# A planner's rule for short transfers beside weight loads, and the constants of a list schedule set anew

## The chip, the cores and the metric

The kernel runs on one core of a Trainium2 chip. The metric is the device time of one execution in microseconds (us), the median over several runs. Before the change it is 965.49 us (three runs, 964.73 to 967.22).

## The reference

Eight batches of local attention with a few global positions, and behind them a two-layer feed-forward network with a Mish-like function. Cut to what matters:

```
k_all, v_all = concat(k_g, k_l), concat(v_g, v_l)          # 32 global + 512 local positions, 8 heads of 64
out_g = softmax(q_g k_all^T / 8) v_all                     # global queries see everything
s_ll  = where(|i - j| <= 32, q_l k_l^T / 8, -1e9)          # local queries: a band of 65 ...
out_l = softmax([q_l k_g^T / 8, s_ll]) [v_g; v_l]          # ... and the 32 global keys
x = concat(out_g, out_l) as (8 * 544) rows x 512
h = x @ w_in (512 x 2048);  g = h * tanh(softplus(h));  result = g @ w_out (2048 x 512)
```

The weights arrive as 8-byte floating-point numbers (512 KB for a piece of 128 x 512) and are turned into 4-byte ones on the core. The matrix products are made with pairs of 16-bit numbers (a high and a low part of each operand), three products for one.

## The kernel before, in words

The attention is cut into 128 units: a batch b, a pair of heads hp and a quarter t of the 512 local queries. A unit takes scores on TensorE (`scores`, L621), the masked maximum on VectorE (`row_max`, L635), the exponential on ScalarE (`expo`, L644), a split into high and low parts, a transpose, and the product with V (`pv`, L717), whose result VectorE scales (`x_norm`, L727). The rows are then transposed for the network (`xh`, `xl`). For batch 0 the transposes run on TensorE; from batch 1 on they are DMA transposes.

The product with V needs the V rows in a shifted layout. `v_move` makes it: eight transfers from on-chip memory to on-chip memory for each pair of heads, of 32, 128, 48, 96, 48, 48, 16 and 16 KB, all issued by the sync engine (SP) into the tiles `va` and `vc`. The last three come from `vgf`, the global part.

The network works on 17 blocks of 256 rows (two for each batch, and one of all global rows), eight steps to a block. A step is `m1_mm` (L853, 24 matmuls into `h`), Mish on ScalarE (L896), the split of the result on VectorE (L343, L909), and `m2_mm` (L921, twelve matmuls into `o`).

The weights come in 32 pieces: 0 to 15 of `w_in` (W1), 16 to 31 of `w_out` (W2). Pieces 0 to 4 are loaded by ScalarE's queue, the others by GpSimd's (POOL). Piece k of W1 lands in one of five staging slots, slot k % 5, so piece k + 5 can only be loaded when VectorE has turned piece k (three instructions: `w_bits` L427, `w_sum` L434 and L436). TensorE then makes statistics (`w_stat`, L448). When all 16 pieces are in, `w_norm` (L455) finds the common scale, and `w_split` makes the high and low parts that `m1_mm` and `m2_mm` read. So the first `m1_mm` needs all of W1 turned, and the attention rows of the first half of batch 0.

All instructions are put in order ahead of time by a list scheduler (`Plan.order`). Each task has an engine, a cost in ns, what it depends on, and a rank. The scheduler keeps a model of time for TensorE, VectorE, ScalarE, POOL and SP, and at each step takes the task that can start first, on equal starts the one of lowest rank. The instructions are then emitted in that order, and each engine works off its own list strictly in order: a task whose input is late holds up all behind it on its engine. No rank or cost of the planner is seen by the chip; they only set the order.

The rank is the task's number in the order in which the program names it, or, where `pl.slot` is set, 37 times that slot. The network's tasks get `BOOST` added (`pl.late`), so they yield to attention tasks with which they compete. `S1` says in which slot (one slot is one unit of attention) each step of the network is named: blocks 0 to 3 by `BLOCKS` and `PACE`, blocks from 4 on one step a slot with a lag of `LAGX`. `CONV1`, `RATE1`, `CONV2`, `RATE2` set the slots of the turning of the weights, `FIRST1`, `STEP1`, `FIRST2`, `STEP2` those of their splits, `AHEAD_DMA` how far ahead of its turning a piece's load is ranked, `LOAD1` and `LOADS1` the ranks of the opening loads.

In the planner's model, weight loads occupy a line of their own that ends at `late`, and SP's transfers one that ends at `moved`. A transfer starts at s, costs ns = KB x 2.81, and where the two lines overlap each is made longer by the other (`both`). SP issues at least 620 ns apart (`DMA_MIN`); a transfer is taken as landed 2300 ns after it has left its line. A piece of weights costs 512 x 2.81 = 1439 ns on its line. The lines that the change touches:

```
if e == DMA:
    s = max(moved, t)
    both = min(ns, max(0, late - s - self.DMA_IN))
    late += both
    moved = s + ns + both
```

Of the kernel before, what the change touches and what calls it, by code (L numbers as in the profile page):

```python
# [27 lines left out]
NF = 8  # L28
# [21 lines left out]
class Plan:  # L50
# [7 lines left out]
    LOYAL = 800  # L58
    TABLE = 1283
    COLD = 2  # L60
    DEEP, ISSUE, SOFT, LANES = 5, 450, 600, 8

    def __init__(self):
        self.tasks = []
# [70 lines left out]
    def order(self):  # L135
        N = len(self.tasks)
        left, users = [0] * N, [[] for _ in range(N)]
        for n, t in enumerate(self.tasks):
            both = t[2] | t[3]
            left[n] = len(both)  # L140
            for d in both:
                users[d].append(n)
        free = dict.fromkeys((PE, DVE, ACT, POOL, DMA), 0)
        free[POOL], pool = 6900, "dma"
        queue = {e: [] for e in free}
        start, done, on = [None] * N, [0] * N, [None] * N
        columns = {}
        moved, far, late, hard, soft = 0, [], 0, [], []

        def tensor(t, ns, rows):  # L150

            while ns > 1e-6:
                k = int(t / self.TICK + 1e-9)
                slow = 1 if columns.get(k - 1, 0) >= self.COLUMNS else self.COLD
                d = min(ns * slow, (k + 1) * self.TICK - t)
                columns[k] = columns.get(k, 0) + d * 2.4 * rows
                ns -= d / slow
                t += d
            return t

        def enter(n):
            engs, fn, deps, after, new, pri, rows, table = self.tasks[n]
            for e, ns in engs:
                t = max([done[d] + (self.NEXT[e] if on[d] == e else self.HOP) for d in deps] + [start[a] for a in after] + [0])
                bisect.insort(queue[e], (pri, n, ns, t))

        def first(e):

            best = None
            for pri, n, ns, t in queue[e]:  # L170
                table = self.tasks[n][7]
                t = max(t, free[e])
                if table == "dma":
                    lane = hard if e == ACT else soft
                    t = max(t, far[-self.DEEP] if len(far) >= self.DEEP else 0, lane[-self.LANES] if len(lane) >= self.LANES else 0)
                elif e == DMA:
                    t = max(t, hard[-self.LANES] if len(hard) >= self.LANES else 0)
                elif e == ACT and table not in (None, self.table):
                    t += self.TABLE
                e0 = self.tasks[n][0][0][0]  # L180
                if e0 != e and free[e0] <= t + self.LOYAL:
                    continue
                if best is None or t < best[0]:
                    best = (t, pri, e, n, ns)
                    if t == free[e]:
                        break
            return best

        for n in range(N):
            if not left[n]:  # L190
                enter(n)
        for _ in range(N):
            t, pri, e, n, ns = min(c for c in map(first, free) if c)
            if e == POOL:
                pool = self.tasks[n][7]
            start[n], on[n] = t, e
            if self.tasks[n][7] == "dma":
                s = max(t + self.DMA_IN, late)
                both = min(ns, max(0, moved + self.DMA_IN - s))
                moved += both  # L200
                late = s + ns + both
                far.append(late)
                free[e] = t + (self.ISSUE if e == ACT else self.SOFT)
                done[n] = far[-1] + self.DMA_OUT
                (hard if e == ACT else soft).append(done[n])
                queue[e] = [c for c in queue[e] if c[1] != n]
                for u in users[n]:
                    left[u] -= 1
                    if not left[u]:
                        enter(u)  # L210
                continue
            if e == ACT:
                self.table = self.tasks[n][7] or self.table
            for x, _ in self.tasks[n][0]:
                queue[x] = [c for c in queue[x] if c[1] != n]
            if e == PE:
                ns = tensor(t, ns, self.tasks[n][6]) - t
            if e == DVE and free[POOL] > t and pool != "dma":
                ns += 0.6 * min(ns, free[POOL] - t)
            if e == DMA:  # L220
                s = max(moved, t)
                both = min(ns, max(0, late - s - self.DMA_IN))
                late += both
                moved = s + ns + both
                free[e] = max(t + max(self.DMA_MIN, self.tasks[n][6]), moved - self.DMA_AHEAD)
                done[n] = moved + self.DMA_IN + self.DMA_OUT
                hard.append(done[n])
            else:
                free[e] = done[n] = t + ns
            for u in users[n]:  # L230
                left[u] -= 1
                if not left[u]:
                    enter(u)
        self.start, self.on, self.done = start, on, done
        return sorted(range(N), key=lambda n: (start[n], n))
# [13 lines left out]
def attn_mish_kernel(ctx: ExitStack, tc: tile.TileContext, qt, kt, vm, vg, qg, w1, w2, consts_in, out, w64):  # L249
# [314 lines left out]
    def v_hi(b, hp):  # L564
        vf = ("vf", b, hp)
        pl.add([(ACT, act(512) + 93), (DVE, dve2(512))], 0, lambda e: scaled(e, X[vf][:, :, 0, :], X["vraw", b][:, hp], X["sv", b][:, 1:2]), r=[("vraw", b), ("sv", b)], new=[("vf", vf)])
# [198 lines left out]
    def g_max(b, hp):  # L765
        mx = ("gmx", b, hp)
        pl.add(DVE, 69 + 1.04 * 272, lambda: V.tensor_reduce(
            out=X[mx][:, 0:1], in_=X["g", b, hp][:, :272], axis=AX.X, op=ALU.max), r=[("g", b, hp)], new=[("gmx", mx)])

        def go():  # L770
            across(X[mx], 0)
            V.tensor_scalar(X[mx][:, 2:3], X[mx][:, 0:1], X[mx][:, 1:2], -SCALE, ALU.max, ALU.mult)  # L772
        pl.add(DVE, 330, go, w=[mx])
# [175 lines left out]
    UNITS.sort(key=lambda x: (x[0], x[2] // 2, x[1], x[2]) if x[0] < HALVED else x)  # L949
    steps = [(blk, i) for blk in range(NBLK) for i in range(NF)]  # L950

    BLK2 = 29.169
    BLK3 = 39.967
    LAGX = 19.225
    BLOCKS = [9, 17, max(25, int(BLK2)), max(33, int(BLK3))]
    PACE = 0.79
    S1 = [int(BLOCKS[s // NF] + PACE * (s % NF)) if s < 4 * NF else s + max(18, int(LAGX)) for s in range(len(steps))]
    LAG2 = 2
    LATER = 24
    BOOST = 84.202  # L960

    def at(u):
        return [x for x, v in zip(steps, S1) if v == u]

    def unit(u):
        return UNITS[u] if 0 <= u < NU else None
# [3 lines left out]
    def slot(u):  # L970
# [5 lines left out]

        m, m2, md = (at(u - k) for k in (0, LAG2, LAG2 + 1))
        fu, bu, vu = unit(u + 1), unit(u), unit(u - 1) if u - 1 < LATER else unit(u - 2) if u - 2 >= LATER else None
# [24 lines left out]
        if mv1 and t == (2 if hp == 3 else 1):  # L1003
            v_hi(*n1)
        pl.late = BOOST
        for x in m[:1]:
            m1_mm(*x, 0)
        pl.late = 0
        if t == 2:
            g_scores(b, hp)  # L1010
            g_max(b, hp)
        pl.late = BOOST
        for x in m:
# [24 lines left out]
        if mv1 and t == (2 if hp == 3 else 1):  # L1038
            v_lo(*n1)
        pl.late = BOOST  # L1040
        for x in m2:
# [4 lines left out]
        if t == 3:  # L1046
            g_pv(b, hp)
        pl.late = BOOST
        for x in m2:
# [38 lines left out]

    LAG = 4
    ORDER = "k0 q0 m w0 b w1 w2 k1 q1 w3 w4 k2 q2 k3 q3 g"  # L1090
    LOAD1 = -7.91
    LOADS1 = 0.038
    CONV1 = 1.096
    RATE1 = 0.0
    CONV2 = 2.335
    RATE2 = 0.514
    FIRST1 = 6.564
    STEP1 = 1.0
    FIRST2 = 6.491
    STEP2 = 0.0  # L1100
    AHEAD_DMA = 12.457

    def weights():
        for k in range(32):
            at = CONV1 + RATE1 * k if k < 16 else CONV2 + RATE2 * (k - 16)
            if k >= 5:
                pl.slot = at - AHEAD_DMA
                w_load(k)
            pl.slot = at
            w_bits(k)  # L1110
            w_sum(k)
            if k % 16 >= LAG:
                w_stat(k - LAG)
            if k % 16 == 15:
                pl.slot = -100
                for i in range(k - LAG + 1, k + 1):
                    w_stat(i)
                w_norm(k // 16)
        pl.slot = None
        pl.settle()  # L1120
# [3 lines left out]
    for i, x in enumerate(ORDER.split()):  # L1124
        a, n = x[0], int(x[1:] or 0)
        pl.slot = LOAD1 + LOADS1 * i
        if a == "w":
# [17 lines left out]
    weights()  # L1145
    splits += [(FIRST1 + STEP1 * j, j) for j in range(8)] + [(FIRST2 + STEP2 * j, 8 + j) for j in range(8)]
    splits.sort()
    for u in range(-1, max(S1[-1] + LAG2 + 2, NU + 3)):
        slot(u)
# [57 lines left out]
```

## Time and profile before

| what | value |
|---|---|
| median of three runs | 965.49 us (964.73 to 967.22) |
| the profiled execution: its own time, its span | 969.12 us, 967.3 us |
| mean granted TensorE clock | 0.986 |
| busy: TensorE, VectorE, ScalarE, POOL | 916.4, 571.6, 553.6, 26.8 us |

The profile is of one execution, 3.63 us above the median of the runs; its span is 1.82 us shorter than its own time, which holds the start and the end outside the first and last instruction. Times in the trace are counted from the span's start. In lists of instructions the first number is the start, the second the duration; in square brackets stands how long the engine sat idle before, and what released it. In tables by stretch each engine has its busy time and its count of instructions, then come the granted TensorE clock, the mean share of the 16 DMA engines that was busy, and what they moved.

### The profile page before, as it was taken

The page shows a single profiled execution, that of the slowest core. Times are in us where ns is not written, and L with a number is a line of the kernel's source. Part 1 is how long each engine was busy: PE and PEld are TensorE (multiplying, and loading weights), DVE is VectorE, ACT ScalarE, POOL GpSimd, SP SyncE. Part 2 cuts the span into 40 slices and gives each one's busy share as a digit, 9 for nine tenths or more (in the row PEclk, how much of TensorE's full clock was granted, in tenths as well). Part 3 has the DMA queues.
Part 4 walks back from the last instruction along what each step waited for, and adds up shares of the span by engine and source line. Part 5 has one row for each costly group of instructions (what it writes and reads, how often), then busy time and mean ns, then how long its engine had stood idle before and what let it go on. Part 6 is the DMA issues. An engine that isn't in the chain of part 4 may idle for free.

```text
span 967.3 us, 20582 instructions
## 1 busy us (share of the span) xinstructions
PE 916.4 (95%) x8044; PEld 625.2 (65%) x8044; DVE 571.6 (59%) x1749; ACT 553.6 (57%) x1161; POOL 26.8 (3%) x52
## 2 busy tenths in 40 slices
PE   2569999999899999999999999999999999999997
PEld 1346657667577666666666766676666666666664
DVE  5599887767676775755566555755565552222222
ACT  1446886767676687766676657756775651211111
POOL 5111000000000000000000000000000000000000
PEclk9789999999999999999999999999999999999999
DMA  9865235675877976766465447644553321000000
GB/s 369 278 201 189 65 86 134 131 161 136 182 156 136 183 159 135 170 115 122 86 173 110 110 94 163 125 112 98 116 94 64 85 43 34 22 1 22 1 22 22
DMA packets 214417, 113.74 MB, mean 118 GB/s; under 512 B 181168, under 2 KB 194608, under 8 KB 213296
## 3 DMA queue, kind: packets, MB, share of 16 engines
q1 hardware_dynamic: 209568, 95.39, 44.7%
q0 software_dynamic: 3888, 14.16, 4.1%
q10 hardware_dynamic: 864, 2.88, 0.8%
q8 instruction: 63, 1.03, 0.4%
q14 instruction: 34, 0.28, 0.1%
HBM read 46.32 MB, written 8.91 MB: 57 GB/s over the span
## 4 chain that ended last, share of the span: by engine, by line
PE 81%; DVE 8%; DMA 7%; ACT 2%; issue 1%; SPq 1%; POOL 0%; ACTq 0%; DVEq 0%
PE o L921 34%; PE h L853 34%; PE s L621 5%; PE U L717 4%; PE g L755 2%; PE gu L809 2%; DVE W L434 1%; DMA pt<-ph 1%; DVE W L436 1%; DMA vgraw<-in_vg 1%; DMA gpt<-gph 1%; DMA W<-in_w 1%; DMA va<-vgf 1%; DMA consts<-in_consts 1%; DVE vmx L521 1%
## 5 line engine op out<-in xcount | busy, mean ns | idle before, releaser
L921 PE MATMUL o<-W,G 128*128 128x512 f16 x1632 | 386.3, 379 | 0.6 <-DVE W L498 0.5
L853 PE MATMUL h<-xh,W 128*128 128x256 f16 x2048 | 375.9, 273 | 0.2 <-ACT W L334 0.2
L853 PEld LDWEIGHTS <-W 128*128 128x128 f16 x3264 | 310.9, 98 | 72.6 <-issue 10.4
L853 PE MATMUL h<-xl,W 128*128 128x256 f16 x1024 | 279.6, 273 | 0.0
L921 PEld LDWEIGHTS <-G 128*128 128x128 f16 x1632 | 154.5, 98 | 151.3 <-issue 3.3
L896 ACT ACTIVATE e<-h,c 128x512 f32<-128x512 f32 (+1 forms) x137 | 93.2, 684 | 167.8 <-PE h L853 145.4
L343 DVE TENSOR_SCALAR G<-e,c 128x512 f16<-128x512 f32 (+1 forms) x137 | 66.1, 482 | 178.9 <-ACT e L896 177.9
L644 ACT ACTIVATE P<-P,nm 128x192 f32<-128x192 f32 (+1 forms) x256 | 117.4, 459 | 56.4 <-DVE nm L635 55.6
L635 DVE CUSTOM_DVE_ANT_0 P<-s,consts 128x192 f32<-128x192 f32 (+1 forms) x256 | 87.0, 369 | 37.1 <-PE s L621 32.1
L909 DVE SCALAR_TENSOR_TENSOR G<-e,c,G 128x512 f16<-128x512 f32 (+1 forms) x137 | 102.1, 745 | 3.4
L664 DVE SCALAR_TENSOR_TENSOR ph<-P,ph 128x384 f16<-128x384 f32 (+1 forms) x112 | 64.5, 589 | 37.0 <-ACT ph L341 35.2
L717 PEld LDWEIGHTS <-pt 96*128 96x128 f16 (+1 forms) x1536 | 61.5, 98 | 30.9 <-issue 12.4
L621 PE MATMUL s<-k,q 64*128 64x192 f32 (+1 forms) x512 | 65.7, 373 | 15.0 <-DMA q<-in_qt 13.4
L896 ACT ACT_TABLE_LOAD x56 | 71.8, 1283 | 5.3 <-PE h L853 4.3
L717 PE MATMUL U<-va,pt 128*128 128x64 f16 (+1 forms) x768 | 56.4, 194 | 14.3 <-DMA va<-vgf 8.0
L621 PEld LDWEIGHTS s<-k,q 64*128 64x128 f32 x512 | 44.0, 192 | 31.3 <-issue 23.8
L341 ACT ACTIVATE ph<-P 128x384 f16<-128x384 f32 (+1 forms) x99 | 51.4, 539 | 12.0 <-DMA pt<-ph 10.9
L717 PE MATMUL U<-vc,pt 96*128 96x64 f16 x768 | 55.8, 193 | 0.0
L644 ACT ACTIVATION_READ_ACCUMULATOR P<-P,nm 128x1 f32 x256 | 47.9, 187 | 0.0
L777 ACT ACT_TABLE_LOAD x22 | 28.2, 1283 | 26.7 <-DVE gmx L772 24.8
L644 ACT ACT_TABLE_LOAD x33 | 42.3, 1283 | 0.6
L341 ACT ACTIVATE ob<-o,c 128x512 f32<-128x512 f32 (+1 forms) x34 | 22.8, 672 | 25.8 <-PE o L921 25.7
(114 smaller groups left out, 713.1 us busy)
## 6 DMA issues: line engine op xcount, KB each, us to landing
k<-in_kt SPq DMA_DIRECT2D x32, 320.0 KB, 3.5
W<-in_w POOLq DMA_DIRECT2D x17, 512.0 KB, 7.4
out<-ob SPq DMA_DIRECT2D x33, 256.0 KB, 2.3
q<-in_qt SPq DMA_DIRECT2D x32, 256.0 KB, 3.1
vraw<-in_vm SPq DMA_DIRECT2D x8, 1024.0 KB, 5.9
wraw<-in_w POOLq DMA_DIRECT2D x10, 512.0 KB, 4.2
vc<-vf SPq DMA_DIRECT2D x32, 128.0 KB, 2.5
va<-vf SPq DMA_DIRECT2D x32, 96.0 KB, 2.6
```

Of the source, the lines that this page charges most:

```text
L341: A.activation(out=dst, in_=src, func=AF.Copy, scale=c)
L343: V.tensor_scalar(dst, src, c, None, ALU.mult)
L621: T.matmul(X[s[h]][:, cols(u)], X[q][r, u * 128:(u + 1) * 128], X[k][r, c0:c0 + w], start=True, stop=True)
L635: pl.add(DVE, 155 + 1.04 * w, lambda: V.tensor_tensor_reduce(out=half(P, h, w), in0=X[s][:, cols(t)], in1=mask[:, m0:m0 + w], scale=-SCALE ...
L644: pl.add(ACT, 460, lambda: A.activation(out=half(P, h, w), in_=half(P, h, w), func=AF.Exp, bias=X[nm], scale=-1.0, accum_out=X[sums][:, t, ...
L664: pl.add(DVE, dve(n), lambda: V.scalar_tensor_tensor(p_part(X[ph], t, 1), p_src(X[P], t), PSC, p_part(X[ph], t, 0), ALU.mult, ALU.subtract ...
L717: T.matmul(X[u][:, t, h, :], X[pt][:k, p * 4 + h * 2 + c, :], X[vx][:k, t, vl, h * 64:(h + 1) * 64], start=(n == 0), stop=(n == 5))
L777: pl.add(ACT, 470, lambda: A.activation(out=X[P], in_=X["g", b, hp][:, :272], func=AF.Exp, bias=X[mx][:, 2:3], scale=SCALE, accum_out=X[s] ...
L853: T.matmul(X[h][:, f * TB:(f + 1) * TB], wh(i, wl)[:, off:off + 128], X[x][:, d, o:o + TB], start=(n == 0), stop=(n == 11))
L896: chain(blk, i, ACT, 705, lambda a, z: A.activation(out=X[e][:, a:z], in_=hv(blk, i)[:, a:z], func=AF.Mish, bias=0.0, scale=X[c][:, 0:1]), ...
L909: chain(blk, i, DVE, 668, lambda a, z: V.scalar_tensor_tensor(gp(1, blk, i)[:, a:z], X[e][:, a:z], X["c", blk][:, 2:3], gp(0, blk, i)[:, a ...
L921: T.matmul(X[o], gp(g, blk, i)[:, f, t * 128:(t + 1) * 128], wh(8 + i, wl)[:, f * 512:(f + 1) * 512], start=(i == 0 and n == 0), stop=(i = ...
```

## The change

The planner gets a constant SHORT of 500 ns. While the line of the weight loads reaches more than 500 ns beyond a transfer's start on SP (after the 1300 ns of `DMA_IN`), that transfer costs at least 500 ns; since `both` then holds the same 500 ns again, it takes up 1000 ns of SP's line, and the loads' line is made 500 ns longer. Fifteen constants of ranks and slots have new values. An assertion on the order of steps emits nothing. No instruction is added, removed or resized: only the order in which the engines work may change.

```
-    DEEP, ISSUE, SOFT, LANES = 5, 450, 600, 8
+    DEEP, ISSUE, SOFT, LANES, SHORT = 5, 450, 600, 8, 500
...
             if e == DMA:
                 s = max(moved, t)
+                if late - s - self.DMA_IN > self.SHORT:
+                    ns = max(ns, self.SHORT)
                 both = min(ns, max(0, late - s - self.DMA_IN))
...
-    BLK2 = 29.169
-    BLK3 = 39.967
-    LAGX = 19.225
+    BLK2 = 31.263
+    BLK3 = 37.663
+    LAGX = 18.379
...
-    PACE = 0.79
+    PACE = 0.732
...
+    assert all(a <= z - (n % NF == NF - 1) for n, (a, z) in enumerate(zip(S1, S1[1:])))
...
-    BOOST = 84.202
+    BOOST = 122.269
...
-    LOAD1 = -7.91
-    LOADS1 = 0.038
-    CONV1 = 1.096
-    RATE1 = 0.0
-    CONV2 = 2.335
-    RATE2 = 0.514
-    FIRST1 = 6.564
+    LOAD1 = -9.482
+    LOADS1 = 0.109
+    CONV1 = 1.292
+    RATE1 = 0.142
+    CONV2 = 2.956
+    RATE2 = 0.457
+    FIRST1 = 6.031
     STEP1 = 1.0
-    FIRST2 = 6.491
-    STEP2 = 0.0
-    AHEAD_DMA = 12.457
+    FIRST2 = 5.526
+    STEP2 = 0.179
+    AHEAD_DMA = 11.972
```

## The prediction

> **What bounds the kernel now.** The page says which engine fills the span, and in which slices it does not: TensorE is busy in 95%, and what it lacks lies almost all in the first slices of 24 us, where its granted clock is also below full.
>
> ```profile
> PE 916.4 (95%) x8044; PEld 625.2 (65%) x8044; DVE 571.6 (59%) x1749; ACT 553.6 (57%) x1161; POOL 26.8 (3%) x52
> PE   2569999999899999999999999999999999999997
> PEclk9789999999999999999999999999999999999999
> ```
>
> So the span is 916.4 us of TensorE work and some 51 us in which it stood still, and a change of order can win or lose only such idle time. The table by stretch says what is short there.
>
> ```profile
> 37.00:44.00 7.00, 1.51 (x27) 1.50 (x27) 0.03 (x1) 0.00 (x0) 0.00 (x0) 0.50 0.84 251
> 44.00:63.00 19.00, 12.53 (x102) 8.05 (x101) 17.35 (x42) 5.64 (x14) 1.87 (x4) 0.77 0.64 186
> 63.00:81.00 18.00, 15.53 (x123) 8.63 (x120) 17.70 (x57) 11.40 (x28) 2.89 (x6) 0.97 0.54 187
> 81.00:140.00 59.00, 55.28 (x469) 37.76 (x466) 52.52 (x149) 45.88 (x85) 3.68 (x7) 1.00 0.38 106
> ```
>
> From 37 to 44 us neither VectorE (0.03 us) nor ScalarE does anything, and TensorE starts again only at the end. From 44 to 81 VectorE is full (35.05 of 37 us) and TensorE is not: what VectorE lost before 44 is missing there. The waits and the chain that ended last say what all waited for.
>
> ```profile
> PE U L717 <- DMA va<-vgf: 8.0, 1, 8.0
> 34.59 7.87 DMA va<-vgf
> 42.49 1.45 PE U L717 x24
> 36.02 0.69 DVE L434 SCALAR_TENSOR_TENSOR W<-W 128x512 int32<-128x512 int32 x1
> 43.97 0.43 DVE L727 TENSOR_TENSOR x<-U,rs 128x256 f32<-128x256 f32 x1 [7.25 <-PE U L717]
> ```
>
> One transfer of `v_move` (16 KB, for the first pair of heads) is issued at 34.59 and lands 7.87 us later. The first `pv` stands at the head of TensorE's list, `x_norm` at the head of VectorE's, and behind that the last third of the turning of piece 9. The planner had put them there because it thought the rows would be in.
>
> **The rule for short transfers.** What the planner believes, and what the trace has:
>
> ```profile
> 26.95 0.57 SPq L330 DMA_DIRECT2D va<-vf  x1
> 27.62 0.53 SPq L330 DMA_DIRECT2D vc<-vf  x1
> 28.97 1.76 SPq L330 DMA_DIRECT2D va<-vf  x3
> 30.77 0.59 SPq L330 DMA_DIRECT2D vc<-vf  x1
> 31.81 4.28 SPq L330 DMA_DIRECT2D va<-vgf  x3
> va<-vgf SPq DMA_DIRECT2D x64, 16.0 KB, 1.8
> va<-vgf SPq DMA_DIRECT2D x8, 16.0 KB, 4.2
> ```
>
> The last two rows are the same kind of transfer over the whole span and in the window 26 to 60: 1.8 and 4.2 us to landing. The old planner gives a 16 KB transfer 45 ns, so eight of them are its 620 ns spacing, 4.96 us. With the rule each takes 1.0 us of line while the loads' line reaches far enough, 8.0 us. So the new plan has the rows of a pair 8 x (1.0 - 0.62) = 3.0 us later. Does the condition hold when they are issued? These are the loads on POOL:
>
> ```profile
> 23.88 0.53 POOL L414 DMA_DIRECT2D wraw<-in_w  x1
> 26.33 0.53 POOL L411 DMA_DIRECT2D W<-in_w  x1 [1.91 <-DVE W L427]
> 29.60 0.53 POOL L411 DMA_DIRECT2D W<-in_w  x1 [2.75 <-DVE W L436]
> 34.27 0.53 POOL L411 DMA_DIRECT2D W<-in_w  x1 [3.58 <-DVE W L427]
> 36.06 0.53 POOL L411 DMA_DIRECT2D W<-in_w  x1 [1.26 <-DVE W L427]
> 45.40 0.54 POOL L411 DMA_DIRECT2D W<-in_w  x1 [8.81 <-DVE rs L726]
> DMA to landing us min/median/max: 3.4/7.1/9.0
> ```
>
> One load moves the line by 1.44 us, so alone it holds the condition for less than 1 us after its issue; but each raised transfer lengthens it by 0.5. I replayed the rule by hand at the trace's times (the load at 23.88 and two shortly before it already hold the line): it held for about seven of the first ten transfers. So it bites, not always.
>
> What can the hole take in? VectorE had that third of piece 9 waiting, and pieces 10 and 11, whose loads (26.33, 29.60) land by 35.3 and 38.6 at the latest time of the row above (9.0). Piece 12 (34.27) lands at 41.4 by the median of 7.1, piece 13 (36.06) at 43.2. In the dense stretch a piece costs the distance between two of its first instructions:
>
> ```profile
> 55.30 0.42 DVE L427 TENSOR_SCALAR W<-W 128x512 int32<-128x512 int32 x1
> 56.84 0.42 DVE L427 TENSOR_SCALAR W<-W 128x512 int32<-128x512 int32 x1
> 62.37 0.28 DVE L455 CUSTOM_DVE_ANT_0 wd<-ws,consts 128x128 f32<-128x128 f32 x1
> 80.90 0.27 PE L853 MATMUL h<-xh,W 128*128 128x256 f16 x1
> ```
>
> 1.54 us. So 0.7 + 2 x 1.54 = 3.8 us of work are surely at hand, 5.3 us with piece 12. The load at 45.40 (piece 14) waits for VectorE too: turned at 37, piece 9 frees its slot 8 us sooner, so the loads would not run dry behind it. The price of this edit is therefore a gain between 3.0 us (the planner's shift alone) and 7.25 us (the whole hole). I take 4.5, between the 3.8 and the 5.3, since the order that a planner with half the true lateness writes will use some of that work and not all. It counts in full for the end: W1 is complete at 62.37, the first `m1_mm` is at 80.90, and VectorE is full to there; from 81 to 140 TensorE lacks only 3.7 us, so an early start is not used up by a later wait of the same size. If that cover is gone (the filler sits elsewhere in VectorE's list) the gain is nothing.
>
> [...]
>
> **The ranks of the weights.** The turning of W1 moves from slot 1.10 for all pieces to 1.29 + 0.142 k: 7 ranks later for piece 0, (1.292 + 2.13 - 1.096) x 37 = 86 for piece 15. W2 starts 23 ranks later and ends 9 earlier; W1's splits come half a slot sooner. VectorE has the same instructions in another order. With 35.05 of 37 us busy the sum cannot move, only which of them are in first. Bounds: a slot of attention work on VectorE ahead of the last pieces (2.8 us, worked out below) later, the same earlier; I take 0. The opening loads keep their order on their queues: 0. The loads on POOL only change ranks among themselves: 0, within the same bounds.
>
> **The blocks.** Blocks 0 and 1 keep their slots but for one step each; block 2 goes from slot 29 to 31, block 3 from 39 to 37, all from block 4 on one slot sooner (19 to 18). `BOOST` goes up by 38 ranks, one slot of 37: from block 4 on the two cancel. Blocks 0, 1 and 2 yield more: one, one and three slots. What such a slot costs if TensorE cannot fill it is read from the steady part:
>
> ```profile
> 200.00:300.00 100.00, 95.98 (x954) 66.41 (x953) 66.96 (x234) 68.73 (x165) 0.65 (x1) 1.00 0.72 155
> 200.00:300.00 100.00, 39.65 (x336) 31.58 (x336) 1.00 0.72 155
> 200.00:300.00 100.00, 37.26 (x162) 15.02 (x161) 1.00 0.72 155
> 200.00:300.00 100.00, 8.77 (x72) 5.90 (x72) 1.00 0.72 155
> 200.00:300.00 100.00, 7.94 (x18) 1.00 0.72 155
> 200.00:300.00 100.00, 8.99 (x12) 1.00 0.72 155
> ```
>
> All; then the lines L853, L921, L621 (72 score matmuls, four to a unit: 18 units), L343 and L909. Attention alone takes (95.98 - 39.65 - 37.26) / 18 = 1.1 us of TensorE and (66.96 - 7.94 - 8.99) / 18 = 2.8 us of VectorE a unit. Without a network step beside it a unit would leave TensorE idle for 1.7 us. Today it is idle for 4.0 us in this stretch. The bounds are -4.0 (all of that gone) and 5 x 1.7 = +8.5 (all five slots empty). I take 0: a rank decides only between tasks that are ready together, so a step that yields still runs when TensorE has nothing else.
>
> **The sum.** -4.5 + 0 + 0 against the profiled 969.12 us gives 964.6; the profile is 3.6 above the median of the runs, so beside those it is 965.5 - 4.5 = **961.0 us**.
>
> The Trainium skill ("TensorE: Matmul & The Clock Gate", What's actually happening) says that an idle window of about 3.4 us drops TensorE to half its clock. The row 37 to 44 agrees: 0.50. By that rule a filled hole would also shorten matmuls that ran at 0.77 from 44 to 63, by up to 12.53 x 0.23 = 2.9 us; since VectorE sets the pace there, the sum leaves it out.
>
> **The rivals.**
>
> *More (956.5).* The new order fills the whole hole, and the stretch after it runs without its pauses: -7.25, and half of the 4.0 idle us of 200 to 300 go too, -9. For it: all three compute engines were still from 37 to 44. Against: the planner still believes in less than the true lateness (3.0 of 7.9).
>
> *The same (965.5).* The wait moves: loads that are issued sooner (piece 14 at 37, not at 45.40) fill the DMA engines, which were at 0.64 from 44 to 63, just when the rows of the second to fourth pair go out, and `pv` waits there. A load takes 7.1 us to land, so one such wait of 4 to 5 us takes back the gain. Against: the later pairs made TensorE wait for nothing in the old order. The skill's sentence that all queues' transfers interleave on the same 16 engines ("DMA: Bandwidth & Descriptors", Issuing engines are not separate DMA queues) is this rival's ground.
>
> Also here: the rule hardly changes the order, since it did not hold for all transfers, and 965.5 stays.
>
> *Slower (969.5).* The network yields too much. Blocks 0 to 2 start later by their five slots and TensorE, with attention alone, is paced by VectorE at 2.8 us a unit: +8.5 - 4.5 = +4.0. For it: VectorE is busy in 52.5 of the 59 us from 81 to 140, where the first blocks run. It decides once more than 4.5 / 1.7 = 2.6 slots stay empty.
>
> **How the numbers follow.** My forecast has 0.46, with a range of its own of 957.5 to 963.5; more 0.09; the same 0.25; slower 0.20. The range that holds 8 in 10 reaches from the case of more to that of slower: 956.0 to 969.5. A measurement of this kernel tells about 0.3% (2.9 us) from no change, so faster is below 962.6: 0.09 and most of the 0.46, and a little of the same, 0.53. Within: 0.27. Above 968.4: 0.20.
>
> **What would show it.** Right: no engine-wide hole before 60 us; `va<-vgf` is no longer the longest wait of TensorE, or is below 4 us; the last W1 instruction (L455) at about 58, the first `m1_mm` near 76.5, and TensorE's idle time down by as much by 140 us. Wrong: a wait for `va`, `vc` or the loads of 5 us or more elsewhere before 80 (the same), or idle TensorE between 80 and 260 with fewer `h` matmuls than before (slower). If the hole is gone and the span is not shorter, my claim that VectorE's lost time counts in full is what fails.

## The result, and the profile after

The kernel after takes 975.69 us (median of four runs, 975.16 to 978.04), the kernel before beside it 965.51 (964.73 to 967.22): a ratio of 1.0108 [1.0087, 1.0129]. It is 10.2 us slower, where 961.0 was forecast and 956.0 to 969.5 was the range. The profiled execution after is typical of its runs (975.66 us).

The page of the kernel after, its first lines and the rows of the slices of 24 us:

```profile
span 973.9 us, 20571 instructions
PE 919.4 (94%) x8044; PEld 625.2 (64%) x8044; DVE 570.2 (59%) x1742; ACT 550.0 (56%) x1162; POOL 28.0 (3%) x52
PE   2677899998999999999999999999999999999997
PEclk9779999999999999999999999999999999999999
```

TensorE is busier than before in the second and third slice (6 and 7 where it had 5 and 6) and less in the fourth, fifth and tenth (7, 8, 8 where it had 9 or more). So something was won early, and more was lost behind it. The table by stretch of the kernel after, with the columns as in the prediction:

```profile
37.00:44.00 7.00, 5.03 (x37) 3.25 (x38) 3.72 (x9) 0.37 (x1) 1.06 (x2) 0.50 1.05 330
44.00:63.00 19.00, 13.61 (x121) 9.54 (x120) 18.68 (x53) 8.98 (x25) 2.50 (x4) 0.77 0.69 213
63.00:81.00 18.00, 14.72 (x124) 8.59 (x123) 17.74 (x58) 10.73 (x29) 2.81 (x5) 0.91 0.59 195
81.00:140.00 59.00, 52.38 (x409) 33.95 (x408) 45.55 (x121) 42.02 (x73) 2.56 (x5) 0.97 0.31 80
```

The hole is filled: VectorE works 3.72 us of 37 to 44 (0.03 before), TensorE 5.03 (1.51). But from 81 to 140 TensorE stands still for 6.6 us, where it lacked 3.7, and VectorE has 7 us less work there: it waits too. The waits of TensorE and the instructions of the kernel after that answer to the prediction's two marks (L457 is the old L455, L855 the old L853):

```profile
PE U L719 <- DMA va<-vgf: 1.9, 1, 1.9
58.60 0.27 DVE L457 CUSTOM_DVE_ANT_0 wd<-ws,consts 128x128 f32<-128x128 f32 x1
76.57 0.41 DVE L729 TENSOR_TENSOR x<-U,rs 128x256 f32<-128x256 f32 x1
82.19 0.27 PE L855 MATMUL h<-xh,W 128*128 128x256 f16 x1
```

The wait for the first rows is 1.9 us instead of 8.0, and W1 is complete at 58.60 instead of 62.37, almost as forecast. Yet the first `m1_mm` starts at 82.19, later than the 80.90 of before, and not at 76.5. What lies between is counted by the last third of a turned piece (L438; L436 before), from W1's completion to the `x_norm` of the fourth pair of heads (76.57; 75.17 before). After and before, in this order:

```profile
58.60:76.57 17.97, 3.94 (x6) 0.81 0.57 174
```

```profile
62.37:75.17 12.80, 2.15 (x4) 0.94 0.49 170
```

Six pieces of W2 were turned there, against three (the fourth of the lower row began at 61.77, before W1 was complete). Three more at the measured 1.54 us are 4.6 us of VectorE, more than the 3.8 us by which W1 was sooner, and they stand ahead of the attention rows for which the first `m1_mm` has to wait as well. From that `x_norm` to the first `m1_mm` it is 5.7 us before and 5.6 after, so the delay of the rows is carried on. That these pieces are what held the rows is read from the order on VectorE; no run takes them out.

To place the loss of 10 us a typical execution of before is wanted, since the one shown above was a late one. The kernel before was profiled twice more (964.2 and 965.76 us, spans 962.4 and 964.0). Its table in the first of them, and that of the kernel after:

```profile
0.00:60.00 60.00, 28.70 (x203) 18.45 (x204) 41.94 (x114) 17.72 (x47) 17.58 (x33) 0.88 0.91 310
60.00:140.00 80.00, 73.68 (x613) 48.14 (x612) 72.32 (x212) 59.68 (x119) 6.69 (x13) 0.99 0.41 121
140.00:400.00 260.00, 255.59 (x2495) 177.53 (x2493) 181.88 (x612) 188.76 (x426) 1.35 (x3) 1.00 0.72 154
```

```profile
0.00:60.00 60.00, 31.54 (x236) 20.79 (x236) 46.80 (x125) 19.36 (x53) 19.85 (x35) 0.88 0.93 327
60.00:140.00 80.00, 69.28 (x537) 43.67 (x538) 66.23 (x189) 55.54 (x108) 5.94 (x11) 0.94 0.38 106
140.00:400.00 260.00, 249.86 (x2445) 172.84 (x2444) 176.19 (x599) 181.52 (x414) 1.05 (x3) 1.00 0.73 150
```

TensorE's idle time, stretch length less busy time: 31.3 and 28.5 us to 60 (won 2.8), 6.3 and 10.7 to 140 (lost 4.4), 4.4 and 10.1 to 400 (lost 5.7): 7.3 us more in all. The other 4 of the 11.5 us between the two spans are longer busy time: 919.4 against 915.4 us for the same 8044 matmuls (917.4 in the second of the two profiles of before). The granted clock is 0.94 against 0.99 in the middle row.

### The profile page after: what moved, and what is told of

It reads as the page before. It is cut to its first block, busy times and chain, and to the rows that moved or that the text cites. A ratio compares the mean times of both kernels' runs of the same rounds, so it can differ in the third digit from the quotient of the medians.

```text
span 973.9 us, 20571 instructions
## 1 busy us (share of the span) xinstructions
PE 919.4 (94%) x8044; PEld 625.2 (64%) x8044; DVE 570.2 (59%) x1742; ACT 550.0 (56%) x1162; POOL 28.0 (3%) x52
## 4 chain that ended last, share of the span: by engine, by line
PE 74%; DMA 10%; DVE 9%; ACT 4%; SPq 2%; issue 1%; POOL 0%; ACTq 0%; DVEq 0%
PE o L923 31%; PE h L855 30%; PE s L623 4%; PE U L719 4%; DMA gpt<-gph 3%; DMA pt<-ph 2%; PE gu L811 2%; PE g L757 1%; DMA vraw<-in_vm 1%; SPq L332 1%; DVE vmx L523 1%; DVE W L438 1%; DMA va<-vgf 1%; DVE W L436 1%; DMA W<-in_w 1%
## 5 line engine op out<-in xcount | busy, mean ns | idle before, releaser
L855 PE MATMUL h<-xh,W 128*128 128x256 f16 x2048 | 375.1, 273 | 0.4 <-ACT W L336 0.3
L855 PEld LDWEIGHTS <-W 128*128 128x128 f16 x3264 | 310.4, 98 | 71.2 <-issue 8.7
L855 PE MATMUL h<-xl,W 128*128 128x256 f16 x1024 | 279.2, 273 | 0.0
L345 DVE TENSOR_SCALAR G<-e,c 128x512 f16<-128x512 f32 (+1 forms) x133 | 64.1, 482 | 200.1 <-ACT e L898 199.7
L343 ACT ACTIVATE ph<-P 128x384 f16<-128x384 f32 (+1 forms) x106 | 55.2, 539 | 11.3 <-DMA pt<-ph 10.3
```

What stands on the lines that cost most here:

```text
L343: A.activation(out=dst, in_=src, func=AF.Copy, scale=c)
L345: V.tensor_scalar(dst, src, c, None, ALU.mult)
L855: T.matmul(X[h][:, f * TB:(f + 1) * TB], wh(i, wl)[:, off:off + 128], X[x][:, d, o:o + TB], start=(n == 0), stop=(n == 11))
```

## The experiments

Each ratio is against the kernel before on the same chip, with its 95% interval.

### The rule alone, the constants alone

`e1_rule_only`: the rule, with all fifteen constants as before.

```
-    DEEP, ISSUE, SOFT, LANES = 5, 450, 600, 8
+    DEEP, ISSUE, SOFT, LANES, SHORT = 5, 450, 600, 8, 500
...
+                if late - s - self.DMA_IN > self.SHORT:
+                    ns = max(ns, self.SHORT)
```

> The rule with all old constants. Theory A (the old constants were good only for the old order of the start; the rule alone already unsettles the plan): slower than before, 970 or more. Theory B (the loss comes from the network's new ranks, BOOST and the block starts): the wait for va (8.0 us before) shrinks to 1.9 or so as in the changed kernel, TensorE's idle time by 60 us falls from 34 to some 28.5 us, and the run is 961 to 966. Theory C (the loss comes from the later ranks of the weights): as B, 961 to 966.

`e2_constants_only`: the new constants, with the rule never true.

```
-    DEEP, ISSUE, SOFT, LANES, SHORT = 5, 450, 600, 8, 500
+    DEEP, ISSUE, SOFT, LANES, SHORT = 5, 450, 600, 8, 1000000000
```

> All new constants, the rule never true. A: near before, 964 to 968, if the new constants are harmless without the rule. B and C: slow, 973 or more, and the hole of 37 to 44 us is back, so even above the changed kernel's 975.7.

Measured: the rule alone 972.97 us, 1.0083 [1.0064, 1.0102]; the constants alone 984.48 us, 1.0209 [1.0187, 1.0231]. Both lose, by 8 and 20 us, and together they lose 10: the prices do not add. In the rule alone the wait for the first rows is down to 1.9 us as well, and still its first `m1_mm` is at 87.3; with the constants alone the wait is back (5.4 us). So closing the hole is not what decides, and the rule is no gain that the constants spoil.

### Which constants

`e3_old_network`: after, with the old values of the network's ranks (five lines, written here as one). `e4_old_weights`: after, with the old values of the other ten constants, those of the weights (LOAD1, LOADS1, CONV1, RATE1, CONV2, RATE2, FIRST1, FIRST2, STEP2, AHEAD_DMA).

```
-    BLK2, BLK3, LAGX, PACE, BOOST = 31.263, 37.663, 18.379, 0.732, 122.269
+    BLK2, BLK3, LAGX, PACE, BOOST = 29.169, 39.967, 19.225, 0.79, 84.202
```

> The changed kernel with the old BLK2, BLK3, LAGX, PACE and BOOST. B: the loss is gone, 961 to 966, idle TensorE from 200 to 300 us back from 7.7 to about 4.0 us. C: still 972 or more, the idle 7.6 us between 60 and 100 stay (4 before).

> The changed kernel with the old ranks of the weights (LOAD1 to AHEAD_DMA). C: the loss is gone, 961 to 966, TensorE no longer waits 18.0 us for the turning of the weights. B: still 972 or more, with the idle time of 200 to 300 us.

Measured: 975.95 us, 1.0118 [1.0088, 1.0147], and 975.14 us, 1.011 [1.0095, 1.0125]. Neither group, set back, brings anything back. So neither the yielding network nor the ranks of the weights holds the loss by itself; with either group set back, the order that comes out is still about 10 us longer.

### The start of the new order, or the rest of it

With the old constants two orders were planned, one with the rule and one without. `e5_start_of_rule` takes from the first all that its planner starts up to just past the first `x_norm` (some 165 tasks), and then the rest in the order of before. `e6_rest_of_rule` does the reverse.

```
+    def merged(self):
+        plans = []
+        for self.SHORT in (self.FIRST_SHORT, self.REST_SHORT):
...
+        head = [n for n in a if start[n] < self.CUT]
+        taken = set(head)
...
+        return head + [n for n in b if n not in taken]
```

> Old constants. The order is that of the plan with the rule up to just behind the first x_norm (some 165 tasks), and behind it the order of the kernel before for all that is left. Theory D (the gain of the start is real, and what the rule loses is lost by the later order, from 60 us on): TensorE waits at most 2 us for va, and the run is 960.5 to 963.5. Theory E (what VectorE makes up before 44 us is not what the first m1_mm waits for, so nothing of it reaches the end): 964 to 967, with the hole gone all the same.

> Old constants. The order of the kernel before up to just behind the first x_norm, then that of the plan with the rule. D: the wait for va of 8 us is back and the later loss stays, 974 to 977. E: as the rule alone, 971 to 975.

Measured: the rule's start 965.63 us against 966.29, 0.9996 [0.9979, 1.0012]; the rule's rest 975.06 us, 1.0088 [1.0065, 1.0112]. The row of 60 to 140 of the start alone, then of the rest alone:

```profile
60.00:140.00 80.00, 74.07 (x609) 48.44 (x607) 72.15 (x212) 59.54 (x119) 6.70 (x13) 0.96 0.42 121
```

```profile
60.00:140.00 80.00, 66.53 (x536) 42.88 (x536) 69.33 (x193) 52.81 (x100) 6.84 (x12) 0.89 0.41 122
```

With the order of before behind it, the rule's start costs nothing (5.9 us idle, as in the typical execution of before) and brings nothing, though it cuts the wait for the rows to this:

```profile
PE U L732 <- DMA va<-vgf: 1.0, 1, 1.0
```

But the shorter wait is not a shorter start: TensorE is idle for 31.5 us to 60 us, as in the typical execution of before (31.3), and W1 is complete at 61.1. What it no longer waits for the rows it waits elsewhere, so this run doesn't price the hole; the next ones do.

The whole loss of the rule comes back with the order that the planner writes behind the start: 13.5 us idle in this stretch. This kernel also keeps the long wait (9.4 us for the first rows), so a part of that row is the hole's.

### The price of the hole by itself

`e7_pieces_ahead` is the kernel before with its finished order, in which only the turning of the W1 pieces 9, 10 and 11 is moved ahead of the first `x_norm`: the gain of the prediction, without a new plan. `e9_pieces_again` is the same, timed in more rounds; `e10_pieces_9_13` moves pieces 9 to 13.

```
+    def pulled(self):
+        order = self.order()
+        at = order.index(self.first_x)
+        early = [n for n in order[at:] if n in self.pull]
+        return order[:at] + early + [n for n in order[at:] if n not in self.pull]
```

> The kernel before; in its finished order the turning of pieces 9, 10 and 11 is moved ahead of the first x_norm, nothing else. The prediction's own term by itself: VectorE fills 3.8 us of its hole. D: the last W1 instruction (L455 there) comes 3 to 4 us sooner and the run is 961 to 963. E: the same L455, but the first m1_mm stays near 80.9 and the run at 964 to 967.

> The same kernel as e7 (pieces 9 to 11 ahead of the first x_norm), in more runs. Its profile had L455 at 59.0 and the first m1_mm at 77.5, 3.4 us sooner than before. If those 3.4 us reach the end (D): 1.5 to 4.5 us below before, the interval of the ratio wholly under 1. If not (E): within 1 us of before.

> As e7, with pieces 12 and 13 ahead of the first x_norm too. D: L455 up to 7 us sooner than before, the run 3 to 7 us below before. E: the attention rows come later by what the two pieces take (3 us), the first m1_mm no sooner than in e7, the run at that of e7 or up to 2 us above it.

Measured: 964.78 us, 0.9992 [0.9972, 1.0012]; again 965.5, 0.9995 [0.9979, 1.0012]; five pieces 965.5, 1.0000 [0.9983, 1.0016]. The edit did what it should: in 37 to 44 VectorE works 5.64 us in this kernel (the first row) and 2.15 in the typical execution of before.

```profile
37.00:44.00 7.00, 3.60 (x32) 2.57 (x32) 5.64 (x12) 0.37 (x1) 1.24 (x3) 0.50 1.06 305
```

```profile
37.00:44.00 7.00, 3.40 (x32) 2.57 (x32) 2.15 (x7) 0.37 (x1) 0.88 (x2) 0.50 0.91 238
```

So that the start could be compared over several executions, both kernels were profiled again without other edits: before as `e13_before_1` and `e14_before_2`, the moved pieces as `e16_pieces_1` and `e17_pieces_2`.

> The kernel before once more, for its profile. If the profiled execution of before was typical: the wait for va is 7 to 9 us, L455 at 62 to 63, the first m1_mm near 81, and TensorE's idle time by 140 us near 40. If it was a late one: some of these are 2 us or more sooner, or the execution loses less after 300 us.

> The kernel before a third time, for its profile: the same two cases as for e13. If the profiled execution was typical, wait for va 7 to 9 us and L455 at 62 to 63; if not, sooner by 2 us or more, or less lost after 300 us.

> The kernel of e7 once more, for its profile. D': TensorE has lost 3 to 4 us less than before by 140 us and gives it back between 140 and 400. E': its start is no sooner than that of other executions of before.

> The kernel of e7 a further time, for its profile: the same two cases as for e16, idle time by 140 us 3 to 4 us less than in the executions of before and given back by 400 us, or no less than there.

Times: 964.2 and 965.76 us before, 965.81 and 964.04 with the pieces ahead. Completion of W1 and the wait for the first rows in the two of before (each fence one execution; the first of the two starts in a row is the one meant):

```profile
L455 DVE CUSTOM_DVE_ANT_0 wd<-ws,consts x2: 276/280/284, 60.5 to 106.3; 128x128 f32<-128x128 f32 x2
PE U L717 <- DMA va<-vgf: 5.4, 1, 5.4
```

```profile
L455 DVE CUSTOM_DVE_ANT_0 wd<-ws,consts x2: 274/279/284, 61.7 to 107.7; 128x128 f32<-128x128 f32 x2
PE U L717 <- DMA va<-vgf: 6.3, 1, 6.3
```

and in two with the pieces ahead, the earliest and the latest of four:

```profile
L462 DVE CUSTOM_DVE_ANT_0 wd<-ws,consts x2: 272/278/283, 59.0 to 103.9; 128x128 f32<-128x128 f32 x2
PE U L724 <- DMA va<-vgf: 5.2, 1, 5.2
```

```profile
L462 DVE CUSTOM_DVE_ANT_0 wd<-ws,consts x2: 274/279/284, 60.6 to 106.4; 128x128 f32<-128x128 f32 x2
PE U L724 <- DMA va<-vgf: 7.0, 2, 6.2
```

With the 62.4 of the first profile, W1 of before is complete at 61.5 on average of three executions, with the pieces ahead at 59.8 of four (59.0, 60.1, 59.5, 60.6): 1.7 us sooner. The first `m1_mm` is at 80.0 and 78.3, again 1.7. At the end of the kernel the difference is -0.5 us (0.9995), with an interval from -2.0 to +1.2 us: no gain is shown, and one of 1.7 us isn't excluded, but the prediction's 4.5 is. So it is open whether any of the 1.7 us is lost between 78 us and the end. With five pieces moved the start is no better than before: W1 is complete at 61.6 and the first `m1_mm` at 80.1, and TensorE waits up to 4.7 us for a late `x_norm` instead.

### Another order, for a reason that has nothing to do with the change

If any new plan costs as much as this one, then the loss is not the rule's and not the constants'. `e8_hop_175` is the kernel before with the planner's time for a hand-over between engines 5 ns longer; `e11_boost_90` is the kernel before with six ranks more of `BOOST`; `e12_after_hop_175` is the kernel after with the same 5 ns.

```
-    HOP = 170
+    HOP = 175
```

> The kernel before with HOP (the planner's price of a handover between engines) at 175 instead of 170 ns: no rule, no constant of the change, but another order of about as many instructions as with the rule alone. Theory F (the loss is not that of the rule or of any one constant; the order before is an outlier that any new plan gives up): 969 to 976. If the loss is the rule's own: 963 to 968.

```
-    BOOST = 84.202
+    BOOST = 90.202
```

> The kernel before with BOOST at 90.202 instead of 84.202, a step of six ranks. F (any new order loses what the old constants had won): 969 to 980. If BOOST had a smooth effect: a sixth of the change's step of 38 ranks, within 2 us of before.

> The changed kernel with HOP at 175 instead of 170. F: the changed kernel is itself an ordinary order, so another one near it lies on either side, 970 to 982. If the rule and its constants hold a loss of their own, apart from the order: 975 to 977 again.

Measured: 978.16 us, 1.0113 [1.0085, 1.0142]; 976.95 us, 1.0126 [1.0103, 1.0149]; 989.14 us, 1.025 [1.0227, 1.0272]. Five nanoseconds in the planner's idea of a hand-over cost as much as the whole change. The rows of the first, then of the second:

```profile
60.00:140.00 80.00, 68.24 (x560) 44.92 (x559) 69.73 (x207) 56.45 (x111) 6.60 (x13) 0.95 0.43 124
140.00:400.00 260.00, 251.46 (x2412) 173.60 (x2411) 177.74 (x593) 184.29 (x414) 1.54 (x3) 1.00 0.67 144
```

```profile
60.00:140.00 80.00, 73.94 (x629) 48.48 (x628) 73.55 (x215) 59.38 (x118) 6.74 (x13) 0.98 0.43 122
140.00:400.00 260.00, 248.89 (x2386) 172.24 (x2385) 172.09 (x583) 180.23 (x410) 1.06 (x3) 0.98 0.67 145
PE U L717 <- DMA pt<-ph: 8.9, 6, 3.3
```

Neither edit touches the start: by operation and tiles, VectorE's list is that of before until 77 us in the first and 88 us in the second. Each order loses somewhere else: the first in both stretches (11.8 and 8.5 us idle against 6.3 and 4.4), the second is like before to 140 and loses everything behind it (11.1 us). There TensorE waits 8.9 us for the probabilities that SP's queue transposes by DMA, where the typical execution of before has this:

```profile
PE U L717 <- DMA pt<-ph: 3.3, 4, 1.6
PE gu L809 <- DMA gpt<-gph: 0.7, 1, 0.7
```

In the kernel after the same two waits, from 140 to 400 us, are

```profile
PE U L719 <- DMA pt<-ph: 5.8, 4, 2.6
PE gu L811 <- DMA gpt<-gph: 3.9, 5, 1.5
```

9.7 against 4.0 us: in this stretch that is as much as the 5.7 us that it lost.

### Whether the transposes are what the new orders have wrong

If these orders lose because the planner counts on the transposes too early, a planner that believes them 800 ns later should write a good one. `e19_late_turns` is the kernel before with that, `e20_after_late_turns` the kernel after.

```
-                done[n] = moved + self.DMA_IN + self.DMA_OUT
+                done[n] = moved + self.DMA_IN + self.DMA_OUT + (800 if self.tasks[n][6] > 1 else 0)
```

> The kernel before; its planner believes that each transpose by DMA on SP (pt, gpt, xh, xl) is in 800 ns later than before. In the new orders so far, much of what is lost from 140 to 400 us is TensorE's wait for pt and gpt (after 9.7 us, before 4.0). Theory A, these orders are bad because the planner counts on the transposes too early: pt and gpt waits of 140 to 400 fall below 4 us, and the ratio is 1.004 or less. Theory B, any new plan loses, wherever its times are moved: waits and gaps elsewhere, 1.008 to 1.025, as for the eight new plans before it.

> The kernel after with the same 800 ns. Theory A: the waits for pt and gpt from 140 to 400 fall from 9.7 us to below 4 and the ratio against before falls from 1.011 to 1.005 or less. Theory B: the ratio stays between 1.008 and 1.025, with the loss in other places.

Measured: 981.21 us, 1.0165 [1.0133, 1.0197], and 982.57 us, 1.0173 [1.0138, 1.0208]. TensorE's longest waits from 140 to 400 us, of the first and of the second:

```profile
PE U L717 <- DMA pt<-ph: 8.1, 4, 5.8
PE h L853 <- ACT e L896: 2.6, 1, 2.6
PE gu L809 <- DMA gpt<-gph: 1.6, 2, 1.3
```

```profile
PE h L855 <- ACT e L898: 7.3, 2, 6.8
PE U L719 <- DMA pt<-ph: 2.9, 3, 1.5
PE gu L811 <- DMA gpt<-gph: 1.9, 1, 1.9
```

That theory fell. In the kernel before, the waits for transposes go up, from 4.0 to 9.7 us, though the planner now counts on them later. In the kernel after they go down from 9.7 to 4.8 us, and a wait of the network for ScalarE (`e`, 7.3 us) stands in their place; the time gets longer. The late transposes are where some of the orders lose, and not why new orders lose.

## Why the prediction was wrong

**The sign failed at the price of the reordering: "I take 0: a rank decides only between tasks that are ready together" and "VectorE has the same instructions in another order".** The first of these is true of each single choice; what failed is to price it at 0. The planner writes one fixed list for each engine. By its code a changed time or rank shifts the starts, and with them the choices, of all that comes behind, and on the chip an instruction at the head of a list holds up all that stand behind it, ready or not (VectorE for 7.25 us in the hole). Ten new plans were run, the whole change and nine with a part of it, with nothing of it, or with something besides (e1, e2, e3, e4, e8, e11, e12, e19, e20); all are slower than before, by 0.8 to 2.5%, which is 8 to 24 us. The prediction bounded each constant by what its own tasks could lose (-4.0 to +8.5 us for the blocks, 2.8 us either way for the weights); the price belongs to the plan as a whole, and it outweighs the term by far. The sum lacked a term for "another order behind the start"; in these ten plans, three of which have nothing of the change, it came to +8 to +24.

**The one term, -4.5, was mis-sized: it is about -0.5, and hardly more than -2.** Its first half was right. The hole was a wait for late rows, work for VectorE was at hand, and with it moved ahead W1 is complete sooner. Two things shrink it, and a third may. First, the hole was read from one execution, in which the wait was 8.0 us; in two others of the same kernel it is 5.4 and 6.3. Second, of 3.5 us of work moved into 37 to 44 (5.64 less 2.15), 1.7 us arrive at W1's completion and at the first `m1_mm`. Third, of those 1.7 us some 0.5 arrive at the end, with an interval that holds both 0 and 1.7.

**"It counts in full for the end" fell as the prediction itself had put it.** The hole is gone and the span is not shorter. In the kernel after, the time saved on VectorE never reached the first `m1_mm` (82.19 against 80.90): the planner's list has three more pieces of W2 in that place. The prediction followed W1 to the first `m1_mm` and left out of its sum that the attention rows of the same half batch had to be there too, and stood on the same engine behind those pieces.

**The clock.** The prediction read the 0.50 of the row 37 to 44 as the work of the hole, and put up to 2.9 us, outside its sum, on filling it. The kernel after has the hole filled, and its rows 37 to 44 and 44 to 63 have the same 0.50 and 0.77. Before the change the clock was down ahead of the hole: the same four matmuls take 0.39 us at 29.65 and 0.61 at 33.92, behind an idle time of 2.20 us.

```profile
29.65 0.39 PE L448 MATMUL ws<-W 128*128 128x128 bf16 x4
33.92 0.61 PE L448 MATMUL ws<-W 128*128 128x128 bf16 x4 [2.20 <-DVE W L436]
```

**The marks.** No hole of all engines before 60 us: right. The wait for `va` below 4 us: right, 1.9. W1 complete at about 58: right, 58.6. The first `m1_mm` near 76.5: wrong, 82.2. Idle TensorE down by 140 us: wrong; 39.2 us to there, against 37.6 in the typical execution of before.

**The rivals.** More: no, the kernel with the hole filled by hand is at 0.9995. The same, by a wait that moves or an order that hardly changes: no, the run is clear of no change, and the order does change. Slower, by a network that yields too much: the sign is right and the mechanism is not, since with the old constants of the network the kernel stays at 975.95 us, and the rule alone at 972.97.

**What stays open.** Why the order of before is better than all ten others. The stretch is common to their losses: from 60 to 400 us TensorE is idle for 16.8 to 29.8 us in the ten, and for 10.7 to 12.0 in three executions of before, which is more than half of each loss. But no one wait is: it is transposes in some and ScalarE in others. A rival that no run here tests is that the constants of before had been chosen because their order happened to be fast; then nearly any other plan would be slower, and the loss would say little about the change.

## What to carry to other kernels

Where a planner writes the order for engines that work strictly in turn, an edit of its times or ranks is a new plan, and its price cannot be had from the part that was edited: re-plan with a constant moved by next to nothing first (here three such plans cost 11 to 16 us), and take the spread of those times as the bound. To judge the idea itself, make the move in the finished order and leave the rest of it as it is; here that showed that the hole was worth some 0.5 us, at most about 2, and not 4.5. And measure a hole over several executions before pricing it, and follow what the freed engine does next up to every input of the instruction that is to start sooner.

## What the runs showed of the hardware that was not expected

The same 16 KB transfer beside the same loads made the first `pv` wait for 8.0, 5.4 and 6.3 us in three executions of one kernel. TensorE's granted clock fell to half without a long pause: in the kernel after it is 1.00 from 35.0 to 35.5 us and 0.50 from 35.75 on, and the longest idle time of TensorE from 21 us to there is 1.49 us. The profile that the prediction rests on was unlucky in a second place, too: around 330 us its granted clock fell to 0.85 (the first row), and in the next profile of the same kernel it did not (the second).

```profile
330.00:340.00 10.00, 8.27 (x96) 6.84 (x94) 7.64 (x24) 9.14 (x20) 0.00 (x0) 0.85 0.85 139
```

```profile
330.00:340.00 10.00, 9.66 (x110) 7.14 (x108) 8.22 (x32) 8.93 (x23) 0.00 (x0) 1.00 0.94 182
```
